# A rebuilt prologue in a fused attention and feed-forward kernel: load order, mask by matmul, a first stage begun operand by operand

## The chip, the cores and the metric

The kernel runs on one core of one Trainium2 chip. The metric is the device time of one execution in microseconds (us); lower is better. The span of a profile is the time from the first to the last instruction of one execution, about 2 us less than the device time. All runs compared below are fast; one run of the kernel before was slow and is left out.

The engines are PE (matmul), PEld (its weight loads), DVE (vector), ACT (scalar), POOL (GpSimd) and SP (which only issues DMA here). "Granted clock" is the share of full speed at which PE was allowed to run. PSUM is the memory in which this kernel keeps the tiles that its matmuls write.

## The reference, cut to what matters

There are 8 batches, 8 heads, 576 positions and a head size of 64. Attention is the sum of two parts: one over positions averaged in fours, and a local one over a band of seven positions. A feed-forward network with a gated activation follows.

```python
q_d = q.reshape(B, H, S // 4, 4, D).mean(axis=3)       # k_d and v_d alike
out_up = np.repeat(softmax(scale * q_d @ k_d.T) @ v_d, 4, axis=2)
mask = np.abs(pos[:, None] - pos[None, :]) < 4
out_local = softmax(np.where(mask, scale * q @ k.T, -1e9)) @ v
x = (out_up + out_local).transpose(0, 2, 1, 3).reshape(4608, 512)
h = x @ w_in                                            # 512 -> 2048
return (h * sigmoid(1.702 * h)) @ w_out                 # 2048 -> 512
```

## The kernel before

The kernel works in nine groups of 512 tokens. Each group runs `mm1` (64 `hps` matmuls with w_in), then `mm2` (64 `ops` matmuls with w_out), and the attention of the next batch is woven into those matmuls. Batch 0 has no group to hide in: its attention is the prologue, and everything up to the first full-speed `hps` matmul is exposed.

v is loaded by the SP queue in ten transfers of 128 KB, each made of rows of 64 floats, which is 256 bytes. q, k and both weights are loaded by the GpSimd queue, with a cast to bf16.

```python
def load_v(b, gate=None):
    t = ldp.tile([128, 5, H, D], FP32, name="vf", tag="vf")
    ...
    for i in range(5):
        for par in range(2):
            nc.sync.dma_start(out=t[64 * par : 64 * par + 64, i],
                in_=bass.AP(tensor=v.tensor, offset=...,
                            ap=[[D, 64], [S * D, H], [1, D]]))
```

v is issued first. GpSimd pools q and k itself and casts half of v, and issues the rest of the weights only behind that.

```python
load_v(0)
load_qk(0, 0)
...
pool_qk(0, 0)                       # GpSimd averages k and q in fours
sp = scores(0, 0)                   # local scores, 80 matmuls
exp_local(0, sp)
...
load_w_in(0, 512)
sd = scores_d(0, 0)                 # pooled scores, 24 matmuls
exp_down(0, sd)
mask_local(0)                       # multiply by the mask on DVE
...
prep_v(0, nc.scalar, ...); prep_v(0, nc.vector, ...); prep_v(0, nc.gpsimd, ...)
load_w_in(512, 512); load_w_in(1024, 1024); ...; load_w_out(0)
...
for hp in range(4):
    x[hp] = transp(y[hp])           # three PSUM buffers in turn
    merge(0, hp, x[hp], copy_od(x[hp]), ...)   # writes xT, the input of mm1
load_v(1, gate=gate)
```

An output tile leaves PSUM through one of three `osb` buffers and is stored by the SP queue, which also loads v.

The softmax here doesn't subtract the row's maximum and nothing guards it: scores larger than these inputs give would overflow.

Of the kernel before, what the change touches and what calls it, by code (L numbers as in the profile page):

```python
# [19 lines left out]
def kernel(  # L20
# [31 lines left out]
    psA = ctx.enter_context(  # L52
        tc.tile_pool(name="psA", bufs=3, space=bass.MemoryType.PSUM)
    )
    psM = ctx.enter_context(
        tc.tile_pool(name="psM", bufs=2, space=bass.MemoryType.PSUM)
# [13 lines left out]

    wz = consts.tile([128, 512], BF16, name="wz")
    psel = consts.tile([128, 7, 64], BF16, name="psel")
# [40 lines left out]
    def make_mask():  # L113
        nc.vector.tensor_tensor(out=dm, in0=dm, in1=dm, op=ALU.mult)
        nc.vector.tensor_single_scalar(out=dm, in_=dm, scalar=9.5, op=ALU.is_lt)
        nc.scalar.copy(
            out=mask.rearrange("p x (i c) -> p (x i) c", c=60),
            in_=dm[:, None, :].to_broadcast([128, 10, 60]),
        )
# [167 lines left out]
    def ps_tile(name):  # L287
        return psA.tile([128, 2, 512], FP32, name=name, tag="psA")

    def scores(b, qd):  # L290
        sp = [ps_tile("sl0"), ps_tile("sl1")]
        for i in range(5):
            for a in range(2):
                for par in range(2):
                    for r in range(4):
# [7 lines left out]
                            start=(a == 0), stop=(a == 1),  # L303
                            tile_position=(32 * r, 64 * par),
                        )
        return sp

    def scores_d(b, qd, sd=None):
        sd = sd or ps_tile("sd")
        for kc in range(3):  # L310
            for a in range(2):
                for r in range(4):
                    rows = slice(32 * r, 32 * r + 32)
                    j = r % 2
                    nc.tensor.matmul(  # L315
                        sd[64 * j : 64 * j + 64, r // 2, SD * kc : SD * kc + SD],
                        lhsT=kdT[qd][rows, 48 * kc : 48 * kc + 64, a],
                        rhs=qdT[b, qd][rows, :, a],
                        start=(a == 0), stop=(a == 1),
                        tile_position=(32 * r, 64 * j),  # L320
                    )
        return sd
# [19 lines left out]
    def av(b, hp):  # L342
        o = ps_tile("av")
# [51 lines left out]
    def transp(y):  # L395
        x = ps_tile("xt")
# [64 lines left out]
    def warm(n):  # L461
        if n:
            t = psM.tile([128, 512], FP32, name="warm", tag="psM")
# [5 lines left out]
    def attention(b):  # L469
# [19 lines left out]
        def avn(*hps):  # L489
            def f():  # L490
                for hp in hps:
                    st["o", hp] = av(b, hp)
# [4 lines left out]
        def tr(*hps):  # L497
            def f():
                for hp in hps:
                    st["x", hp] = transp(st["y", hp])  # L500
# [6 lines left out]


    def mm1(g, steps):
        tok0 = g * TG  # L510
        gT = moe_sb.tile([128, n_ffc, TG], BF16, name="gT", tag="gT")
        for ffc in range(n_ffc):
            for f in steps.get(ffc, ()):
                f()
            hps = psM.tile([128, TG], FP32, name="hps", tag="psM")
            for dmc in range(n_dmc):
                nc.tensor.matmul(  # L517
                    hps,
                    lhsT=w_in_bf[:, dmc, ffc * 128 : (ffc + 1) * 128],
                    rhs=xT[dmc][:, tok0 : tok0 + TG],  # L520
                    start=(dmc == 0), stop=(dmc == n_dmc - 1),
                )
            nc.scalar.activation(  # L523
                out=gT[:, ffc, :], in_=hps, func=AF.Silu, scale=GELU_SCALE
            )
        return gT

    def mm2(g, gT, steps):
# [3 lines left out]
        if g == 0:  # L532
            order = [(t0 + u, c * 4 + f) for t0 in (0, 2) for c in range(4)
# [16 lines left out]
        for t, ffc in order:  # L550
# [5 lines left out]
            if ffc == 0:  # L556
                ops[t] = psM.tile([128, d_model], FP32, name="ops", tag="psM")
# [9 lines left out]
        if g == n_groups - 1:  # L567
            for h in range(2):
                cols = slice(256 * h, 256 * h + 256)
                p = psM.tile([128, d_model], FP32, name="ops", tag="psM")  # L570
# [151 lines left out]
```

## Time and profile before

| | before |
|---|---|
| device time, median of 3 | 336.61 us (334.76 to 338.91) |
| profiled span | 336.2 us |
| PE busy, mean granted clock | 94%, 0.974 |
| first y (a head pair's attention result) | 22.54 us |
| last xT (input of the first stage) complete | 31.47 us |
| first mm2 matmul | 45.96 us |
| group 1's first hps matmul | 74.34 us |
| group 1's first mm2 matmul | 89.58 us |

The first view is the page of the kernel before. Its first line gives busy time, share of the span and number of instructions of each engine. The others cut the span into 40 slices of 8.4 us each; a digit is the busy share, or the granted clock, in tenths.

```profile
PE 315.9 (94%) x5013; PEld 157.4 (47%) x5013; DVE 135.3 (40%) x217; ACT 184.2 (55%) x315; POOL 138.6 (41%) x164
...
PE   6777993999999999999999999999999999999995
...
PEclk9699996799999999999999999999999999999999
DMA  8899992199991897199519951898180010011012
```

PE is full from the eighth slice on. All that a new prologue can win lies in the first eight, where PE is at 0.6 to 0.9 and once at 0.3, and the clock falls twice. The busy time there is not all useful: it includes dummy `warm` matmuls on zeros, whose results nothing reads.

The next view is the table by stretches of the kernel before. Its columns are the stretch in us, its length, busy us and number of instructions of PE, PEld, DVE, ACT and POOL, the granted clock, the DMA share and GB/s.

```profile
10.00:12.50 2.50, 2.14 (x103) 1.59 (x106) 1.26 (x1) 1.23 (x2) 2.10 (x3) 0.78 1.20 220
12.50:15.00 2.50, 2.42 (x98) 1.18 (x88) 2.38 (x3) 1.00 (x2) 2.42 (x3) 0.50 0.84 151
15.00:17.50 2.50, 2.50 (x21) 0.91 (x23) 2.50 (x3) 1.12 (x2) 2.42 (x4) 0.50 0.05 8
20.00:25.00 5.00, 3.53 (x149) 2.28 (x145) 2.67 (x5) 2.08 (x2) 2.62 (x5) 1.00 1.17 189
50.00:55.00 5.00, 0.01 (x1) 0.04 (x1) 0.00 (x0) 0.08 (x1) 1.06 (x1) 0.74 0.49 80
```

DMA is busy until about 14.5 us, nearly idle from 15 to 17.5 us, then busy again. From 50 to 55 us PE does nothing.

The last view is the timeline of the kernel before: start, us from the first start to the last end, engine and line, operation, output and inputs, count, and in brackets the idle time ahead and what ended it.

```profile
0.74 12.28 SPq L174 DMA_DIRECT2D vf<-in_v_dram  x10
...
16.23 0.80 POOL L196 DMA_DIRECT2D w_in_bf<-in_moe_w_in_dram  x1
...
17.04 0.93 PE L315 MATMUL sd<-qdT_281,kdT_98 32*64 32x144 bf16 x24
...
22.54 1.09 DVE L389 TENSOR_TENSOR y<-av,rc 128x896 bf16<-128x896 f32 x1
...
30.51 0.75 DVE L446 TENSOR_TENSOR xT_85<-xt,od 128x570 bf16<-128x570 f32 x1 [0.22 <-ACT od L425]
...
53.94 2.32 POOL L251 CAST vb_87<-vf 128x2560 bf16<-128x2560 f32 x1 [13.12 <-DMA vf<-in_v_dram]
...
56.32 1.71 PE L272 MATMUL vdp<-vb_87,psel 128*64 128x256 bf16 x14 [6.31 <-POOL vb_87 L251]
```

v is issued at 0.74 us and w_in at 16.23 us. The PE stall of 6.31 us waits for v of batch 1, which landed at 53.9 us behind the weights.

### The profile page before, as it was taken

How to read it: one execution, taken by the hardware profiler on the slowest of the kernel's cores; microseconds unless marked ns; L12 is line 12 of the kernel's file. 1: busy time of each engine (PE TensorE's matmuls, PEld its weight loads, DVE VectorE, ACT ScalarE, POOL GpSimd, SP SyncE). 2: the span in 40 equal slices, each digit the busy share in tenths (PEclk: the TensorE clock that was granted, in tenths of full speed). 3: DMA queues.
4: the chain of work that ended last, by engine and by line, in shares of the span. 5: the costliest groups of instructions: out<-in, count | busy, mean ns of one | idle time of the engine just before them, and what ended most of it. 6: DMA issues, size and time to landing. Idle time of an engine off the chain costs nothing.

```text
span 336.2 us, 11213 instructions
## 1 busy us (share of the span) xinstructions
PE 315.9 (94%) x5013; PEld 157.4 (47%) x5013; DVE 135.3 (40%) x217; ACT 184.2 (55%) x315; POOL 138.6 (41%) x164
## 2 busy tenths in 40 slices
PE   6777993999999999999999999999999999999995
PEld 2343442454545455545554545455545554444444
DVE  5766710384067506750675066506750570000000
ACT  2346760546664667466746673668366737424611
POOL 6966802027940892089208920793079000000000
PEclk9699996799999999999999999999999999999999
DMA  8899992199991897199519951898180010011012
GB/s 148 150 159 211 196 200 42 67 181 198 262 190 68 164 204 139 64 181 204 120 67 188 204 114 66 161 208 135 66 163 13 33 67 31 2 63 62 0 55 71
DMA packets 63552, 41.36 MB, mean 123 GB/s; under 512 B 44048, under 2 KB 54416, under 8 KB 63504
## 3 DMA queue, kind: packets, MB, share of 16 engines
q1 hardware_dynamic: 55056, 26.95, 37.5%
q0 software_dynamic: 8304, 13.63, 23.0%
q8 instruction: 39, 0.64, 0.8%
q14 instruction: 9, 0.07, 0.1%
q10 hardware_dynamic: 144, 0.07, 0.1%
HBM read 44.83 MB, written 9.44 MB: 161 GB/s over the span
## 4 chain that ended last, share of the span: by engine, by line
PE 84%; SPq 5%; DMA 4%; POOL 2%; DVE 2%; issue 1%; ACT 1%; POOLq 0%; ACTq 0%
PE ops L558 36%; PE hps L517 33%; SPq L174 5%; DMA qb_128<-in_q_dram 2%; PE sd L315 2%; PE av L354 2%; PE xt L403 2%; PE av L376 2%; DMA vf<-in_v_dram 1%; PE ops L572 1%; PE vdp L272 1%; POOL vb_87 L251 1%; PE warm L465 1%; DVE y L389 1%; PE xt L413 0%
## 5 line engine op out<-in xcount | busy, mean ns | idle before, releaser
L558 PE MATMUL ops<-w_out_bf,gT 128*128 128x512 bf16 x560 | 129.8, 383 | 0.0
L523 ACT ACTIVATE gT<-hps 128x512 bf16<-128x512 f32 x144 | 86.0, 597 | 49.0 <-PE hps L517 49.0
L517 PEld LDWEIGHTS <-w_in_bf 128*128 128x128 bf16 x576 | 55.8, 98 | 68.4 <-issue 2.0
L558 PEld LDWEIGHTS <-gT 128*128 128x128 bf16 x560 | 52.2, 98 | 60.8 <-issue 2.1
L517 PE MATMUL hps<-xT_85,w_in_bf 128*128 128x512 bf16 x144 | 54.6, 379 | 0.8 <-DVE vf L590 0.8
L517 PE MATMUL hps<-xT_82,w_in_bf 128*128 128x512 bf16 x144 | 54.6, 379 | 0.0
L517 PE MATMUL hps<-xT_84,w_in_bf 128*128 128x512 bf16 x144 | 54.6, 379 | 0.0
L517 PE MATMUL hps<-xT_83,w_in_bf 128*128 128x512 bf16 x144 | 54.6, 379 | 0.0
L543 ACT ACTIVATE osb<-ops 128x512 f32<-128x512 f32 (+2 forms) x37 | 22.0, 595 | 40.4 <-PE ops L558 27.2
L340 DVE TENSOR_TENSOR es_90<-es_90,mask 128x600 bf16<-128x600 bf16 x8 | 7.6, 950 | 84.8 <-ACT es_90 L326 84.8
L425 ACT COPY od<-xt 128x384 f32<-128x384 f32 x64 | 21.1, 412 | 36.3 <-PE xt L413 30.8
L389 DVE TENSOR_TENSOR y<-av,rc 128x896 bf16<-128x896 f32 x32 | 34.9, 1092 | 1.1
L545 DVE TENSOR_SCALAR osb<-ops 128x128 f32<-128x128 f32 x1 | 0.3, 291 | 55.3 <-ACT osb L543 55.3
L387 DVE RECIPROCAL rc<-av 128x14 f32<-128x14 f32 x32 | 7.7, 240 | 19.6 <-PE av L376 19.6
L465 PE MATMUL warm<-wz 128*128 128x512 bf16 x41 | 14.1, 476 | 1.2 <-DVE wz L100 1.2
L251 POOL CAST vb_87<-vf 128x2560 bf16<-128x2560 f32 x4 | 9.4, 2344 | 13.1 <-DMA vf<-in_v_dram 13.1
L403 PEld LDWEIGHTS <-y 60*64 60x64 bf16 x640 | 7.4, 107 | 9.2 <-issue 4.3
L403 PE MATMUL xt<-ident,y 60*64 60x57 bf16 (+1 forms) x640 | 9.5, 194 | 1.3 <-issue 0.8
L340 DVE TENSOR_TENSOR es_92<-es_92,mask 128x600 bf16<-128x600 bf16 x8 | 4.2, 529 | 13.8 <-ACT es_92 L326 13.8
L482 ACT ACT_TABLE_LOAD x7 | 9.0, 1283 | 0.1
L478 ACT ACT_TABLE_LOAD x7 | 9.0, 1283 | 0.1
L446 DVE TENSOR_TENSOR xT_84<-xt,od 128x570 bf16<-128x570 f32 x8 | 6.0, 754 | 7.1 <-ACT od L425 7.1
(335 smaller groups left out, 382.5 us busy)
## 6 DMA issues: line engine op xcount, KB each, us to landing
vf<-in_v_dram SPq DMA_DIRECT2D x80, 128.0 KB, 6.6
out_dram<-osb SPq DMA_DIRECT2D x35, 256.0 KB, 2.1
v_96<-in_v_dram SPq DMA_DIRECT2D x36, 192.0 KB, 5.4
w_out_bf<-in_moe_w_out_dram POOLq DMA_DIRECT2D x4, 512.0 KB, 18.0
w_in_bf<-in_moe_w_in_dram POOLq DMA_DIRECT2D x2, 512.0 KB, 6.6
w_in_bf<-in_moe_w_in_dram POOLq DMA_DIRECT2D x1, 1024.0 KB, 11.6
kb_116<-in_k_dram POOLq DMA_DIRECT2D x1, 288.0 KB, 5.3
qb_118<-in_q_dram POOLq DMA_DIRECT2D x1, 288.0 KB, 6.7
```

Source lines behind the costliest of these rows:

```text
L174: nc.sync.dma_start(out=t[64 * par : 64 * par + 64, i], in_=bass.AP(tensor=v.tensor, offset=v[b, 0].offset + (114 * i + KSTART[par]) * D, ...
L251: cp(out=vbs[b % 2][:, i, h, 0:D], in_=vf[b][:, i, h])
L340: nc.vector.tensor_tensor(out=ev, in0=ev, in1=mask, op=ALU.mult)
L389: nc.vector.tensor_tensor(out=y, in0=ov[:, :, :, 0:D], in1=rc.to_broadcast([128, 2, 7, D]), op=ALU.mult,)
L403: nc.tensor.matmul(x[64 * j : 64 * j + 64, par, 57 * i + c0 : 57 * i + c1], lhsT=y[64 * pos : 64 * pos + 60, par, i, :], rhs=ident[64 * po ...
L425: nc.scalar.copy(out=od[:, 4 * t0 : 4 * (t0 + n)].rearrange("p (t f) -> p t f", f=4), in_=x[:, xx, 288 : 288 + n, None].to_broadcast([128, ...
L465: nc.tensor.matmul(t, lhsT=wz[:, 0:128], rhs=wz, start=True, stop=True)
L478: nc.scalar.preload_act_table_set("exp_and_others")
L517: nc.tensor.matmul(hps, lhsT=w_in_bf[:, dmc, ffc * 128 : (ffc + 1) * 128], rhs=xT[dmc][:, tok0 : tok0 + TG], start=(dmc == 0), stop=(dmc = ...
L523: nc.scalar.activation(out=gT[:, ffc, :], in_=hps, func=AF.Silu, scale=GELU_SCALE)
L543: eng.activation(out=osb, in_=ap, func=AF.Copy, scale=1.0 / GELU_SCALE)
L558: nc.tensor.matmul(ops[t], lhsT=gT[:, ffc, t * 128 : (t + 1) * 128], rhs=w_out_bf[:, ffc, :], start=(ffc == 0), stop=(ffc == n_ffc - 1),)
```

## The change

The intent is to make the first stage start earlier and to take out the stall near 50 us. q and k are loaded first, and v waits for the first q tile. For batch 0, the local mask is added to the scores by matmuls instead of multiplied in by DVE, and q is not pooled: the pooled scores come from four accumulating matmuls over its four strided quarters. The weights are issued as soon as GpSimd has averaged the second k tile. v of batch 1 comes before half of w_out. Six `hps` tiles of the first stage begin with the operands that are ready, and the first `mm2` runs over four PSUM accumulators at once. The diff, cut to its core:

```diff
-    load_v(0)
     load_qk(0, 0)
...
     prep_1("q", 0, 0)
-    pool_qk(0, 0)
-    sp = scores(0, 0)
+    load_v(0, gate=after_q)                 # v waits for the first q tile
+    pool_qk(0, 0, "k")
+    sp = scores(0, 0, barred=True)          # mask added by bar_others(), 8 matmuls
     exp_local(0, sp)
     prep_qk(0, 1)
-    pool_qk(0, 1)
+    pool_qk(0, 1, "k")
     load_w_in(0, 512)
...                                          # from below, behind prep_v, to here:
     load_w_in(512, 512)
     load_w_in(1024, 1024)
     for qd in range(NQ):
         load_qk(1, qd)
     load_w_out(0)
+    load_w_out(1)
...
-    sd = scores_d(0, 0)
+    sd = scores_d(0, 0, pooled=False)       # 96 matmuls instead of 24
     exp_down(0, sd)
-    mask_local(0)
...
+    for i in range(5):
+        prep_v(0, nc.vector, i=slice(i, i + 1))
...
+    turned(0)                               # transp + merge, all through PSUM slot 2
+    y[2] = normalise(av(0, 2, 0))
+    part((0, 1), 0)                         # two hps tiles, operand 0
+    turned(1)
+    y[3] = normalise(av(0, 3, 1))
+    part((0, 1), 1)
+    turned(2)
+    part((2, 3), 0, 1)
+    part((0, 1), 2)
+    turned(3)
+    part((4, 5), 0, 1)
+    part((2, 3, 4, 5), 2)
+    part(range(6), 3)
...
-            order = [(t0 + u, c * 4 + f) for t0 in (0, 2) for c in range(4)
+            order = [(t0 + u, 4 * c + f)
+                     for t0, c in ((0, 0), (0, 1), (2, 0), (2, 1),
+                                   (0, 2), (2, 2), (0, 3), (2, 3))
                      for u in range(2) for f in range(4)]
```

The unpooled scores read q like this:

```diff
+        q_of = [qdT[b, qd]] if pooled else [
+            qT[b, qd].rearrange("p (t f) a -> p t f a", f=4)[:, :, f, :]
+            for f in range(4)
+        ]
```

A row of qT holds two bf16 values per position, and a matmul takes one of the two.

More of the change, by code (lines that the diff above doesn't have):

```diff
@@ L51 @@
     moe_sb = ctx.enter_context(tc.tile_pool(name="moe_sb", bufs=1))
-    psA = ctx.enter_context(
-        tc.tile_pool(name="psA", bufs=3, space=bass.MemoryType.PSUM)
-    )
-    psM = ctx.enter_context(
-        tc.tile_pool(name="psM", bufs=2, space=bass.MemoryType.PSUM)
+    psum = ctx.enter_context(
+        tc.tile_pool(name="psum", bufs=1, space=bass.MemoryType.PSUM)
     )
@@ L69, with ps_tile, pm_tile @@
     kdT = [persist.tile([128, 160, 2], BF16, name=f"kdT{i}") for i in range(NQ)]
+    PA = [psum.tile([128, 2, 512], FP32, name=f"pa{i}") for i in range(3)]
+    PM = [psum.tile([128, 512], FP32, name=f"pm{i}") for i in range(2)]
+    turn = {"a": 0, "m": 0}
+    def ps_tile(n=None):
+        if n is None:
+            n = turn["a"] % 3
+            turn["a"] += 1
+        return PA[n]
+    def pm_tile():
+        turn["m"] += 1
+        return PM[turn["m"] % 2]
     wz = consts.tile([128, 512], BF16, name="wz")
+    off = consts.tile([128, 60], BF16, name="off")
     psel = consts.tile([128, 7, 64], BF16, name="psel")
@@ L115, in make_mask @@
         nc.vector.tensor_single_scalar(out=dm, in_=dm, scalar=9.5, op=ALU.is_lt)
+        nc.vector.tensor_scalar(
+            out=off, in0=dm, scalar1=-1.0, scalar2=1e6, op0=ALU.add, op1=ALU.mult
+        )
         nc.scalar.copy(
@@ L284, in prep_vd_pe, with bar_others, scores @@
         )
-    def ps_tile(name):
-        return psA.tile([128, 2, 512], FP32, name=name, tag="psA")
-    def scores(b, qd):
-        sp = [ps_tile("sl0"), ps_tile("sl1")]
+    def bar_others(sp):
+        for par in range(2):
+            rows = slice(64 * par, 64 * par + 64)
+            for r in range(4):
+                nc.tensor.matmul(
+                    sp[r // 2][rows, r % 2, 0:300],
+                    lhsT=ident[rows, :],
+                    rhs=off[rows, None, :].to_broadcast([64, 5, 60]),
+                    start=True, stop=True,
+                    tile_position=(64 * par, 64 * par),
+                    skip_group_check=True,
+                )
+    def scores(b, qd, barred=False):
+        sp = [ps_tile(), ps_tile()]
+        if barred:
+            bar_others(sp)
         for i in range(5):
@@ L302, in scores, with scores_d @@
                             rhs=qT[b, qd][rows, q0 : q0 + 60, a],
-                            start=(a == 0), stop=(a == 1),
+                            start=(a == 0 and not barred),
+                            stop=(a == 1 or barred),
                             tile_position=(32 * r, 64 * par),
+                            skip_group_check=barred,
                         )
         return sp
-    def scores_d(b, qd, sd=None):
-        sd = sd or ps_tile("sd")
-        for kc in range(3):
-            for a in range(2):
-                for r in range(4):
-                    rows = slice(32 * r, 32 * r + 32)
-                    j = r % 2
-                    nc.tensor.matmul(
-                        sd[64 * j : 64 * j + 64, r // 2, SD * kc : SD * kc + SD],
-                        lhsT=kdT[qd][rows, 48 * kc : 48 * kc + 64, a],
-                        rhs=qdT[b, qd][rows, :, a],
-                        start=(a == 0), stop=(a == 1),
-                        tile_position=(32 * r, 64 * j),
-                    )
+    def scores_d(b, qd, pooled=True):
+        sd = ps_tile()
+        q_of = [qdT[b, qd]] if pooled else [
+            qT[b, qd].rearrange("p (t f) a -> p t f a", f=4)[:, :, f, :]
+            for f in range(4)
+        ]
+        last = len(q_of) - 1
+        for kc in range(3):
+            for f, qq in enumerate(q_of):
+                for a in range(2):
+                    for r in range(4):
+                        rows = slice(32 * r, 32 * r + 32)
+                        j = r % 2
+                        nc.tensor.matmul(
+                            sd[64 * j : 64 * j + 64, r // 2, SD * kc : SD * kc + SD],
+                            lhsT=kdT[qd][rows, 48 * kc : 48 * kc + 64, a],
+                            rhs=qq[rows, :, a],
+                            start=(a == 0 and f == 0), stop=(a == 1 and f == last),
+                            tile_position=(32 * r, 64 * j),
+                        )
         return sd
@@ L340, in mask_local, with av @@
             nc.vector.tensor_tensor(out=ev, in0=ev, in1=mask, op=ALU.mult)
-    def av(b, hp):
-        o = ps_tile("av")
+    def av(b, hp, n=None):
+        o = ps_tile(n)
         av_local(b, hp, o)
@@ L393, in normalise, with transp @@
         return y
-    def transp(y):
-        x = ps_tile("xt")
+    def transp(y, n=None):
+        x = ps_tile(n)
         for i in range(5):
@@ L462, in warm @@
         if n:
-            t = psM.tile([128, 512], FP32, name="warm", tag="psM")
+            t = pm_tile()
             for _ in range(n):
@@ L467, in warm, with attention @@
                 )
-    def attention(b):
+    def attention(b, slots=None):
         st = {}
@@ L490, in f @@
             def f():
-                for hp in hps:
-                    st["o", hp] = av(b, hp)
+                for n, hp in enumerate(hps):
+                    st["o", hp] = av(b, hp, slots and slots[n])
                 for hp in hps:
@@ L498, in f @@
             def f():
-                for hp in hps:
-                    st["x", hp] = transp(st["y", hp])
+                for n, hp in enumerate(hps):
+                    st["x", hp] = transp(st["y", hp], slots and slots[n])
                 for hp in hps:
@@ L506, in attention, with hps_mm, new_gT, silu @@
         return [lambda: s_pe(0), lambda: s_act(0), s1, avn(0, 1), avn(2, 3), tr(0, 1), tr(2, 3)]
-    def mm1(g, steps):
-        tok0 = g * TG
-        gT = moe_sb.tile([128, n_ffc, TG], BF16, name="gT", tag="gT")
-        for ffc in range(n_ffc):
+    def hps_mm(g, ffc, dmc, acc):
+        nc.tensor.matmul(
+            acc,
+            lhsT=w_in_bf[:, dmc, ffc * 128 : (ffc + 1) * 128],
+            rhs=xT[dmc][:, g * TG : g * TG + TG],
+            start=(dmc == 0), stop=(dmc == n_dmc - 1),
+        )
+    def new_gT():
+        return moe_sb.tile([128, n_ffc, TG], BF16, name="gT", tag="gT")
+    def silu(gT, ffc, acc):
+        nc.scalar.activation(
+            out=gT[:, ffc, :], in_=acc, func=AF.Silu, scale=GELU_SCALE
+        )
+    def mm1(g, gT, steps, first=0):
+        for ffc in range(first, n_ffc):
             for f in steps.get(ffc, ()):
                 f()
-            hps = psM.tile([128, TG], FP32, name="hps", tag="psM")
+            hps = pm_tile()
             for dmc in range(n_dmc):
-                nc.tensor.matmul(
-                    hps,
-                    lhsT=w_in_bf[:, dmc, ffc * 128 : (ffc + 1) * 128],
-                    rhs=xT[dmc][:, tok0 : tok0 + TG],
-                    start=(dmc == 0), stop=(dmc == n_dmc - 1),
-                )
-            nc.scalar.activation(
-                out=gT[:, ffc, :], in_=hps, func=AF.Silu, scale=GELU_SCALE
-            )
-        return gT
+                hps_mm(g, ffc, dmc, hps)
+            silu(gT, ffc, hps)
     def mm2(g, gT, steps):
@@ L556, in mm2 @@
             if ffc == 0:
-                ops[t] = psM.tile([128, d_model], FP32, name="ops", tag="psM")
+                ops[t] = PA[0][:, t - 2, :] if g == 0 and t > 1 else pm_tile()
             nc.tensor.matmul(
@@ L569, in mm2 @@
                 cols = slice(256 * h, 256 * h + 256)
-                p = psM.tile([128, d_model], FP32, name="ops", tag="psM")
+                p = pm_tile()
                 for ffc in range(n_ffc):
@@ L586, with after_q, after_w_out @@
     POS = [13, 16, 33, 42, 53, 62, 71]
-    POS_0 = [14, 16, 34, 48, 56, 64, 72]
+    POS_0 = [14, 16, 24, 48, 66, 56, 76]
     gate = lambda t: nc.vector.memset(t, 0.0)
     o, y, x = {}, {}, {}
-    load_v(0)
+    def after_q(t):
+        nc.vector.tensor_copy(out=t, in_=qf[0, 0][0:1, 0:1])
+    def after_w_out(t):
+        nc.vector.tensor_copy(out=t, in_=w_out_bf[0:1, 0, 0:1])
+    nc.scalar.preload_act_table_set("exp_and_others")
     load_qk(0, 0)
-    nc.scalar.preload_act_table_set("exp_and_others")
-    iota_psel()
     load_qk(0, 1)
     iota_mask()
+    iota_psel()
     fill()
     warm(17)
-    make_psel(dp, dr)
     make_mask()
+    make_ident(di)
     prep_1("k", 0, 0)
     prep_1("q", 0, 0)
-    pool_qk(0, 0)
-    sp = scores(0, 0)
+    load_v(0, gate=after_q)
+    pool_qk(0, 0, "k")
+    sp = scores(0, 0, barred=True)
     exp_local(0, sp)
     prep_qk(0, 1)
-    pool_qk(0, 1)
+    pool_qk(0, 1, "k")
     load_w_in(0, 512)
-    warm(3)
-    sd = scores_d(0, 0)
-    exp_down(0, sd)
-    mask_local(0)
-    warm(2)
-    sp = scores(0, 1)
-    exp_local(1, sp)
-    mask_local(1)
-    make_ident(di)
-    warm(5)
-    sd = scores_d(0, 1)
-    exp_down(1, sd)
-    prep_v(0, nc.scalar, i=slice(0, 2), h=slice(0, 4))
-    prep_v(0, nc.vector, i=slice(2, 5), h=slice(0, 4))
-    prep_v(0, nc.gpsimd, h=slice(4, 8))
     load_w_in(512, 512)
@@ L630, with part, turned @@
     load_w_out(0)
+    load_w_out(1)
+    make_psel(dp, dr)
+    sd = scores_d(0, 0, pooled=False)
+    exp_down(0, sd)
     warm(2)
+    sp = scores(0, 1, barred=True)
+    exp_local(1, sp)
+    sd = scores_d(0, 1, pooled=False)
+    exp_down(1, sd)
+    nc.scalar.preload_act_table_set("silu_and_others")
+    for i in range(5):
+        prep_v(0, nc.vector, i=slice(i, i + 1))
+    warm(4)
+    prep_vd_pe(0, PA[2])
     for hp in range(2):
-        o[hp] = ps_tile("av")
+        o[hp] = PA[hp]
         av_local(0, hp, o[hp])
-    prep_vd_pe(0, ps_tile("vdp"))
-    nc.scalar.preload_act_table_set("silu_and_others")
-    warm(2)
-    for hp in range(4):
-        if hp < 2:
-            av_down(0, hp, o[hp])
-        else:
-            o[hp] = av(0, hp)
-        y[hp] = normalise(o[hp])
-    warm(2)
-    for hp in range(4):
-        x[hp] = transp(y[hp])
-        merge(0, hp, x[hp], copy_od(x[hp]), eng=nc.gpsimd if hp < 2 else None)
-        warm(2)
-    load_v(1, gate=gate)
-    for c in range(1, 4):
-        load_w_out(c)
+    for hp in range(2):
+        av_down(0, hp, o[hp])
+        y[hp] = normalise(o[hp])
+    warm(4)
+    gT0 = new_gT()
+    turn["m"] = 0
+    acc = PM + [PA[n][:, u, :] for n in range(2) for u in range(2)]
+    def part(ffcs, *dmcs):
+        for dmc in dmcs:
+            for ffc in ffcs:
+                hps_mm(0, ffc, dmc, acc[ffc])
+    def turned(hp):
+        x[hp] = transp(y[hp], 2)
+        merge(0, hp, x[hp], copy_od(x[hp]))
+    turned(0)
[11 more added lines that the diff above has]
+    part(range(6), 3)
+    for ffc in range(6):
+        silu(gT0, ffc, acc[ffc])
     def loads_2():
-        load_qk(2, 0, gate=gate)
-        load_qk(2, 1)
-        load_v(2)
+        load_v(2, gate=gate)
         load_v4(2)
@@ L661 @@
         if g == 0:
-            prep_1("k", 1, 0)
-            prep_1("q", 1, 0)
+            prep_qk(1, 0)
             pool_qk(1, 0)
@@ L666 @@
             pool_qk(1, 1)
+            load_v(1, gate=after_w_out)
             nc.vector.memset(v4[32:64], 0.0)
-            prep_v(1, nc.gpsimd)
+            prep_v(1, nc.gpsimd, i=slice(0, 4))
+            load_w_out(2)
+            load_w_out(3)
+            prep_v(1, nc.gpsimd, i=slice(4, 5))
+            for qd in range(NQ):
+                load_qk(2, qd)
         elif b < B:
@@ L684 @@
         if b < B:
-            for n, f in zip(POS if g else POS_0, attention(b)):
+            for n, f in zip(POS if g else POS_0, attention(b, None if g else (1, 2))):
                 steps.setdefault(n, []).append(f)
             if g == 0:
-                steps[POS_0[2]].insert(0, lambda: prep_vd_pe(1, ps_tile("vdp")))
-                steps[POS_0[3]].append(loads_2)
-        gT = mm1(g, steps)
+                steps.setdefault(45, []).append(lambda: prep_vd_pe(1, PA[2]))
+                steps[POS_0[5]].append(loads_2)
+        gT = new_gT() if g else gT0
+        mm1(g, gT, steps, 0 if g else 6)
         mm2(g, gT, {n - 16: f for n, f in steps.items() if n >= 16})
```

## The prediction

> **What bounds the kernel now.** The span is 336.2 us, PE busy 94%. From 74.4 us on, the chain of waits is almost only PE: six groups of about 33.8 us, then 58.8 us. The change leaves them alone. All there is to win lies before 74.4 us, where group 1's matmuls start.
>
> The timeline and the table by stretches show four costs there. (1) The last xT comes at 31.5 us; only 3 of group 0's 128 matmuls ran before it. (2) DMA limits what is below: its share is about 1.1 from 2.5 to 14.5 us (q, k, v of batch 0), near 0 to 17.5 because GpSimd issues w_in only at 16.2, then 1.0 to 1.25 until v of batch 1 lands at 53.7. (3) PE idles 50.0 to 56.3 us for the cast vb_87 of that v. (4) The granted clock is then 0.50 to about 62 us: fourteen ops matmuls take 4.5 us, not 3.0. (3) and (4) cost about 9 us. [...]
>
> **What the change does.** It loads q/k first, v behind them; the mask goes into PSUM by 16 matmuls, so four multiplications (5.2 us of VectorE) go; q is not pooled for batch 0 (144 more sd matmuls, 23 to 39 ns each, in PE slack). The w_in issue moves from 16.2 to about 11.5 us. v of batch 1 comes before half of w_out, so it should land near 45 us: (3) and (4) should vanish. Over six hps tiles, 18 matmuls run before the last xT: 15 x 0.216 = 3.2 us won.
>
> VectorE still makes y and xT of four head pairs in series (4 x 1.35 + 4 x 1.0 us), through one PSUM slot, and v lands at 17 to 18 us, so the last xT comes at 30 to 32 us, as before. Six SiLUs in a row (0.6 us each) then hold PE about 1.5 us. The second score step, moved to 8 matmuls into mm2, waits for table load and exponentials: 1.8 us.
>
> **The new wait.** Group 0 now finishes all four output tiles within its last 13 matmuls. From n=40 the SP queue first issues v and v4 of batch 2: 16 issues of at least 0.5 to 0.6 us, 10 to 14 us in all. The first store stands behind them; the fourth osb reuses its buffer (there are three) and stands ahead of all SiLUs of group 1. From that gate to the end of mm2 are about 4.6 us; PE can do two more hps tiles (1.7 us), then waits until the store has landed (2.1 us). I estimate 6.5 to 10 us of PE idle, then about 3 us of slow clock.
>
> **Sum.** Last xT 30.5 + 110 x 0.216 + attention 6.2 + small waits 4 + new wait 8 + clock 3 = 75.5 us, against 74.4. The stall is moved, not removed. My new wait may be too large, so I shade it down.
>
> Predicted: 335.0 us, range 328.0 to 340.0; faster by over 2%: 0.22, within 2%: 0.73, slower by over 2%: 0.05.
>
> **What would show it.** Right: no PE idle for vb near 50 us; first mm2 matmul at 41 to 45 us (46.0 before); ACT's fourth osb waits for the out DMA; PE idles over 5 us after group 1's second hps tile; clock near 0.5 after it; later groups 33.5 us each. Wrong: group 1 flows without that gap (325 to 329 us), or vdp or w_out still stalls mm2.
>
> **What would make it wrong.** v issues faster than 0.5 us each; v of batch 0 landing at 14 us, everything 3 us earlier; the clock low during the split hps matmuls (slower).

The sum comes to 75.5 us: 30.5 + 23.8 + 6.2 + 4 + 8 + 3. The last term, 3 us of slow clock, is an estimate that fits the trace before: after its stall PE ran at a clock of 0.50 for about 6 us (56.3 to 62.5 us), and half of that is lost.

## The result, and the profile after

The changed kernel took 368.15 us (367.23 to 368.45, four runs), the kernel before 337.53 us in the same rounds. The ratio is 1.091, with a 95% interval of 1.086 to 1.097: 9% slower. A ratio here and below is the record's, from the fast runs of the same rounds, so it is not quite the ratio of the medians quoted. The record has no mark of correctness for this run; e1 to e3, which leave its arithmetic as it is, are marked correct. The range of the prediction, 328 to 340 us, missed it by 28 us.

The page after, in slices of 9.1 us:

```profile
PE 329.8 (90%) x5159; PEld 164.4 (45%) x5159; DVE 133.0 (36%) x222; ACT 181.7 (50%) x312; POOL 130.2 (36%) x156
...
PE   8990579899259999999999999999999999999996
...
PEclk9665568999859999999999999999999999999999
DMA  7899400597999017941992497179418011002002
```

There are two holes in PE: slices 4 to 5 (0 and 5), and slices 11 to 12 (2 and 5). DMA is full in the first hole and idle right after it.

The table by stretches after, with the same columns:

```profile
15.00:20.00 5.00, 5.00 (x127) 2.71 (x123) 0.43 (x1) 2.12 (x3) 2.88 (x5) 0.58 1.23 204
...
30.00:35.00 5.00, 0.00 (x0) 0.00 (x0) 0.00 (x0) 0.00 (x0) 0.00 (x0) 0.50 1.16 200
...
40.00:45.00 5.00, 3.31 (x86) 1.97 (x85) 1.92 (x4) 0.80 (x1) 0.00 (x0) 0.50 0.03 6
95.00:105.00 10.00, 0.00 (x0) 0.00 (x0) 2.56 (x3) 1.13 (x3) 9.76 (x12) 0.64 1.10 227
```

From 30 to 35 us no engine works while DMA moves 200 GB/s. From 95 to 105 us PE does nothing. The clock is at 0.50 in and after the first hole and at 0.64 in the second.

The timeline after:

```profile
9.12 6.33 PE L350 MATMUL pa<-qT,kdT 32*64 32x144 bf16 x96
...
11.70 2.36 POOL L211 DMA_DIRECT2D w_in_bf<-in_moe_w_in_dram  x3
...
15.30 0.43 DVE L266 CAST vb<-vf 128x512 bf16<-128x512 f32 x1 [1.53 <-DMA vf<-in_v_dram]
...
26.40 0.43 DVE L266 CAST vb<-vf 128x512 bf16<-128x512 f32 x1 [10.67 <-DMA vf<-in_v_dram]
...
36.25 0.43 DVE L266 CAST vb<-vf 128x512 bf16<-128x512 f32 x1 [9.42 <-DMA vf<-in_v_dram]
...
41.02 0.43 DVE L266 CAST vb<-vf 128x512 bf16<-128x512 f32 x1 [4.33 <-DMA vf<-in_v_dram]
...
43.74 1.09 DVE L424 TENSOR_TENSOR y<-pa,rc 128x896 bf16<-128x896 f32 x1
...
56.18 0.75 DVE L481 TENSOR_TENSOR xT<-pa,od 128x570 bf16<-128x570 f32 x1 [2.38 <-ACT od L460]
...
103.87 0.60 ACT L585 ACTIVATE osb<-pa 128x512 f32<-128x512 f32 x1 [11.96 <-DMA out_dram<-osb]
105.00 1.44 PE L544 MATMUL pm<-xT,w_in_bf 128*128 128x512 bf16 x3 [10.55 <-ACT gT L555]
```

The five casts of v's slices tell the story of the first hole. The second was done at 15.7 us; the third, fourth and fifth waited for their data until 26.4, 36.3 and 41.0 us. w_in had been issued at 11.70 us, between the first request for v and its landing. In the second hole the fourth output tile waits for a buffer whose store has not landed (11.96 us), and PE waits for ACT behind it (10.55 us).

The time from one milestone to the next shows where the 29 us came from:

| stage | before, us | after, us | difference |
|---|---|---|---|
| start to first y | 22.54 | 43.74 | +21.2 |
| first y to last xT complete | 8.93 | 13.40 | +4.5 |
| last xT to first mm2 matmul | 14.49 | 12.78 | -1.7 |
| first mm2 matmul to group 1's first hps | 28.38 | 21.70 | -6.7 |
| group 1's first hps to its first mm2 | 15.24 | 28.19 | +12.9 |
| sum | 89.58 | 119.81 | +30.2 |

The spans differ by 29.2 us; the later groups take 33.4 to 34.4 us each in both kernels. So the intended gains are there (the rows with -1.7 and -6.7), and they are outweighed by three losses.

### The profile page after: what moved, and what is told of

The parts are those of the page before. It is cut to its first block, busy times and chain, and to the rows that moved or that the text cites. A ratio compares the mean times of both kernels' runs of the same rounds, so it can differ in the third digit from the quotient of the medians.

```text
span 365.4 us, 11482 instructions
## 1 busy us (share of the span) xinstructions
PE 329.8 (90%) x5159; PEld 164.4 (45%) x5159; DVE 133.0 (36%) x222; ACT 181.7 (50%) x312; POOL 130.2 (36%) x156
## 4 chain that ended last, share of the span: by engine, by line
PE 77%; DMA 10%; SPq 5%; ACT 3%; DVE 2%; issue 1%; POOL 0%; DVEq 0%; ACTq 0%; POOLq 0%
PE pm L544 33%; PE pm L600 30%; DMA vf<-in_v_dram 6%; SPq L189 4%; PE pa L326 3%; PE pa L438 2%; DMA out_dram<-osb 2%; PE pa L350 2%; PE pa L389 2%; PE pa L411 2%; DMA qb<-in_q_dram 1%; ACT gT L555 1%; DVE xT L481 1%; PE pa L544 1%; PE pa L600 1%
## 5 line engine op out<-in xcount | busy, mean ns | idle before, releaser
L544 PE MATMUL pm<-xT,w_in_bf 128*128 128x512 bf16 x560 | 127.3, 384 | 14.5 <-ACT gT L555 11.1
L600 PE MATMUL pm<-w_out_bf,gT 128*128 128x512 bf16 x528 | 121.3, 380 | 0.0
L555 ACT ACTIVATE gT<-pm 128x512 bf16<-128x512 f32 x140 | 83.3, 598 | 48.9 <-PE pm L544 48.9
L544 PEld LDWEIGHTS <-w_in_bf 128*128 128x128 bf16 x576 | 56.3, 99 | 84.3 <-issue 20.6
L460 ACT COPY od<-pa 128x384 f32<-128x384 f32 x64 | 21.1, 411 | 40.8 <-DVE y L424 22.2
L585 ACT ACTIVATE osb<-pm 128x512 f32<-128x512 f32 (+2 forms) x35 | 20.7, 593 | 40.2 <-PE pm L600 28.3
L424 DVE TENSOR_TENSOR y<-pa,rc 128x896 bf16<-128x896 f32 x32 | 34.9, 1091 | 1.1
L481 DVE TENSOR_TENSOR xT<-pa,od 128x570 bf16<-128x570 f32 x32 | 24.1, 753 | 16.3 <-ACT od L460 16.3
L361 ACT ACTIVATE es<-pa 128x600 bf16<-128x600 f32 x32 | 19.7, 668 | 6.8 <-PE pa L326 6.3
L272 POOL TENSOR_TENSOR v<-v 112x512 f32<-112x512 f32 x18 | 22.8, 1267 | 0.0
L235 DVE STREAM_TRANSPOSE kT<-kb 128x576 f32<-128x576 f32 x16 | 19.9, 1246 | 0.9 <-DMA kb<-in_k_dram 0.9
L235 DVE STREAM_TRANSPOSE qT<-qb 128x576 f32<-128x576 f32 x16 | 19.8, 1238 | 0.2
L367 ACT ACTIVATE ed<-pa 128x864 bf16<-128x864 f32 x16 | 14.3, 896 | 9.9 <-PE pa L350 9.9
L251 POOL TENSOR_TENSOR pq<-qT 128x576 f32<-128x576 bf16 x14 | 16.1, 1147 | 0.0
L350 PEld LDWEIGHTS <-kdT 32*64 32x64 bf16 x528 | 13.6, 114 | 4.2
## 6 DMA issues: line engine op xcount, KB each, us to landing
w_in_bf<-in_moe_w_in_dram POOLq DMA_DIRECT2D x1, 1024.0 KB, 14.5
```

The costliest lines, as they stand in the source:

```text
L235: nc.vector.transpose(out=t32.rearrange("p (i c) -> p c i", c=18), in_=store[b, qd].bitcast(FP32).rearrange("p (c d) -> p c d", c=18),)
L251: nc.gpsimd.tensor_tensor(out=t1, in0=sv[:, :, 0:2, :], in1=sv[:, :, 2:4, :], op=ALU.add)
L272: eng.tensor_tensor(out=t1[0:112], in0=x[:, :, 0:2, :], in1=x[:, :, 2:4, :], op=ALU.add)
L350: nc.tensor.matmul(sd[64 * j : 64 * j + 64, r // 2, SD * kc : SD * kc + SD], lhsT=kdT[qd][rows, 48 * kc : 48 * kc + 64, a], rhs=qq[rows, : ...
L424: nc.vector.tensor_tensor(out=y, in0=ov[:, :, :, 0:D], in1=rc.to_broadcast([128, 2, 7, D]), op=ALU.mult,)
L460: nc.scalar.copy(out=od[:, 4 * t0 : 4 * (t0 + n)].rearrange("p (t f) -> p t f", f=4), in_=x[:, xx, 288 : 288 + n, None].to_broadcast([128, ...
```

## The experiments

The theories, for each hole.

First hole. Theory S: v is starved. Its small rows on the SP queue share the DMA engines with 4.5 MB of bulk on the GpSimd queue, and get a small part. The rivals: v is late of itself, because it is requested behind q and k, in small packets, by ten issues on SP (T); or PE is late because of its 192 pooled-score matmuls, which take 66 ns each where 23 to 39 ns were predicted.

Second hole. Theory W: the first store stands in the SP queue behind sixteen issues for batch 2, and a fourth osb buffer would cure it. The rival: SP and DMA are simply too late there, so that another wait takes its place.

The twelve runs came in three sets, each with its own seven runs of the kernel before: e1 to e4, e5 to e8 and e9 to e12. The first set ran on another chip than the other two, so results of different sets are compared by their ratios. Diffs are against the changed kernel unless the text says otherwise.

### e1_gate: the weights wait for v

```diff
     pool_qk(0, 1, "k")
+    vgate = consts.tile([128, 5], FP32, name="vgate")
+    nc.gpsimd.tensor_copy(out=vgate, in_=vf[0][:, :, 0, 0])
     load_w_in(0, 512)
```

GpSimd copies one value of each slice of v, so its weight loads are issued only when v has landed (from 20.25 us in this run, after the last wait for v at 19.74 us). Everything else stays.

> The changed kernel, with one tiny GpSimd copy that reads the first column of all five slices of v of batch 0, put ahead of the first w_in issue: the bulk loads start only when v has landed. Theory S (v, issued second on another queue, is starved of DMA by the 4.5 MB of w_in, q/k of batch 1 and w_out queued behind it): v lands by 18 us instead of 41, the first y starts near 27 us instead of 43.5 (the unpooled sd matmuls then end last, near 24.6 us), and the time falls by about 16 us, to 349 to 356. Rival T (v is slow of itself: late gate, small packets, ten issues on SP): v still lands after 30 us and the time stays within 1% of 368.

Measured: 354.55 us, ratio 1.051 (1.045 to 1.056), span 352.7 us. The timeline of this run shows v in by 19.7 us, and y 14.3 us earlier than in the changed kernel:

```profile
17.47 0.43 DVE L266 CAST vb<-vf 128x512 bf16<-128x512 f32 x1 [1.11 <-DMA vf<-in_v_dram]
19.74 0.43 DVE L266 CAST vb<-vf 128x512 bf16<-128x512 f32 x1 [1.84 <-DMA vf<-in_v_dram]
...
29.44 1.09 DVE L424 TENSOR_TENSOR y<-pa,rc 128x896 bf16<-128x896 f32 x1
```

v was still requested behind q and k, so the order of the requests is not what cost 21 us. Holding back the bulk alone brought v in 21 us earlier and shortened the span by 12.7 us. v and y both came about 2 us later than expected. And y came 9.7 us after v, not 2.7 us as before the gate. The pooled-score matmuls, which had been hidden, are now in the way; e4 tests that.

### e2_osb4: a fourth output buffer

```diff
-            osb = moe_sb.tile([128, n], FP32, name="osb", tag=f"osb{n}", bufs=3)
+            osb = moe_sb.tile([128, n], FP32, name="osb", tag=f"osb{n}", bufs=4)
```

> The changed kernel with four output buffers in place of three, so that the fourth output copy of group 0 need not wait for the first store, which stands behind 16 loads on the SP queue. Theory W (that buffer is what holds PE from 94.5 to 105 us): the gap of 10.6 us and about 1.5 to 3 us of half clock behind it go, time 354 to 358. Rival: PE is then held by something else at the same place (v of batch 2 late, stores piling up at the next group), and the time falls by less than 5 us.

Measured: 357.64 us (354.71 to 358.11), ratio 1.058 (1.052 to 1.064), span 352.9 us. The same stretches of this run, first the timeline, then the table:

```profile
92.03 10.74 PE L544 MATMUL pm<-xT,w_in_bf 128*128 128x512 bf16 x48 [0.49 <-DVE xT L487]
```

```profile
95.00:105.00 10.00, 9.89 (x145) 4.91 (x145) 1.38 (x2) 6.04 (x11) 9.76 (x12) 1.00 1.07 220
```

The second hole is gone, and with it 12.5 us of the profiled span: 10.55 us of idle and about 2 us of slow clock (0.70 from 105 to 110 us in the changed kernel; 1.00 in the table above). DMA carries the same load there, so it was the buffer and not the DMA rate. The profiled run was the fastest of the four; by medians the gain is 10.5 us.

### e3_gate_osb4: both

The two edits above together.

> Both edits. If the two costs are independent, their savings add: 368 - 16 - 12 = 340, range 335 to 345. If the second gap only reappears elsewhere once the first part is faster, 348 or more.

Measured: 340.68 us, ratio 1.011 (1.005 to 1.017), span 338.7 us. The spans add up within 1.5 us: 365.4 less 12.7 less 12.5 is 340.2. By medians the two gains of 13.6 and 10.5 us give 24.1 us, and both together gave 27.5 us. The two holes are separate, and they are nearly all of the loss. What is left is 1% over the kernel before.

### e4_gate_osb4_pooled: q pooled again

On top of e3:

```diff
-    pool_qk(0, 0, "k")
+    pool_qk(0, 0)
...
-    sd = scores_d(0, 0, pooled=False)
+    sd = scores_d(0, 0)
...                                          # and the same for (0, 1)
```

> Both edits, and q of batch 0 is pooled on GpSimd again, 24 sd matmuls in place of 96 per head group. The 96 took 5.1 to 6.4 us each time in the changed kernel's trace, about 64 ns a matmul. Theory P (once v is in time, they are what the first y waits for): sd is over by 17 us, the first y starts near 21 us instead of 27, time 5 to 7 us below the run with both edits, 332 to 335. Rival (they lie in PE slack, as I predicted): within 2 us of that run.

Where this says 5.1 to 6.4 us, the trace of the changed kernel has 6.33 and 6.38 us for its two 96s, 66 ns a matmul.

Measured: 334.97 us, ratio 0.992 (0.988 to 0.997), span 333.6 us. The timeline of e3, then that of e4:

```profile
9.01 6.33 PE L350 MATMUL pa<-qT,kdT 32*64 32x144 bf16 x96
...
18.08 6.38 PE L350 MATMUL pa<-qT,kdT 32*64 32x144 bf16 x96
```

```profile
10.85 0.58 PE L350 MATMUL pa<-qdT,kdT 32*64 32x144 bf16 x24 [1.70 <-POOL qdT L260]
...
14.88 0.58 PE L350 MATMUL pa<-qdT,kdT 32*64 32x144 bf16 x24 [1.51 <-POOL qdT L260]
...
22.97 1.09 DVE L424 TENSOR_TENSOR y<-pa,rc 128x896 bf16<-128x896 f32 x1
```

Four times the matmuls took eleven times the time. Pooled, PE waits 3.2 us for GpSimd and still finishes 9 us sooner; the first y comes at 22.97 us instead of 29.64 us. This is worth 5.7 us by medians, but only once v is in time: in the changed kernel v came last anyway.

### e5_vfirst: v first, bulk not held back

The fourth buffer, and v requested ahead of q and k as before:

```diff
+    load_v(0)
     load_qk(0, 0)
...
-    load_v(0, gate=after_q)
```

> The changed kernel with four output buffers, and v of batch 0 issued first, ungated, as in the kernel before; w_in is not held back. Theory S (v loses to the bulk loads only because it is still in flight when they start at 12.5 us): v lands by 16 us, time near that of the run with gate and four buffers (340.7), 337 to 345. If the early w_in still starves v's tail, v lands at 20 to 30 us and the time lies between 345 and 357.

Measured: 340.78 us, ratio 1.008 (1.004 to 1.013), span 340.0 us, as fast as e3. Four slices of v were cast by 16.1 us; the fifth, still on its way when the bulk was issued (from 12.84 us), came at 20.65 us, as late as the second theory of the expectation had it, but the time is that of the first. Either remedy serves: bulk behind v by a gate, or v far enough ahead.

### e6_samequeue: v on the queue of the bulk (inconclusive)

The fourth buffer, and v issued by GpSimd between q/k and the weights:

```diff
-                nc.sync.dma_start(
+                (q or nc.sync).dma_start(
...
     iota_mask()
+    load_v(0, q=nc.gpsimd)
```

> The changed kernel with four output buffers, and v of batch 0 issued by GpSimd on the queue that also carries q/k and, behind it, w_in. Nothing is gated. If the loss lies in the sharing between two queues, order within one queue cures it: v lands by 20 us although w_in is queued right behind it, time 340 to 350 (GpSimd pools q/k some 5 us later, which costs). If it lies in v's small packets as such, v lands after 30 us and the time is 355 or more.

Measured: 348.34 us, ratio 1.031 (1.025 to 1.037). This run decides nothing about the queue. GpSimd's ten issues of v (4.4 to 13.1 us) put off its own pooling of k; the pooled scores ran only at 17.1 and 26.2 us, the first y came at 37.5 us. w_in was issued only at 19.07 us, when v was nearly in. So the bulk never met v.

### e7_bulk_over_v: the load order alone, in the kernel before

This is the kernel before, with nothing of the change but the order of the first loads: v behind the first q tile, and the weights right after.

```diff
-    load_v(0)
     load_qk(0, 0)
...
     prep_1("q", 0, 0)
+    load_v(0, gate=lambda t: nc.vector.tensor_copy(out=t, in_=qf[0, 0][0:1, 0:1]))
+    load_w_in(0, 512)                       # these lines come from below
+    load_w_in(512, 512)
+    load_w_in(1024, 1024)
+    for qd in range(NQ):
+        load_qk(1, qd)
+    load_w_out(0)
     pool_qk(0, 0)
```

> The kernel before, with only the order of its first loads changed: q/k first, v of batch 0 on SP gated behind q, and w_in, q/k of batch 1 and the first quarter of w_out issued by GpSimd right behind q/k, ahead of its pooling. Nothing else of the change. Theory S: this alone costs most of the loss: v lands after 35 us, the first y near 40 us instead of 22.5, time 350 to 360. If v lands before 25 us and the time stays below 343, the order of loads is not enough to explain the loss.

Measured: 351.28 us, ratio 1.040 (1.033 to 1.046). v was in at about 36.6 us, the first y came at 41.70 us against 22.54 us. The line of y in its timeline:

```profile
41.70 1.09 DVE L389 TENSOR_TENSOR y<-av,rc 128x896 bf16<-128x896 f32 x1
```

So the load order makes the first hole without the rest of the change. The loss in time, 13.3 us by medians (351.28 less 337.96), is less than the 19 us at the first y; this kernel took 8.9 us from first y to last xT, as the kernel before did, and part of the rest comes back at the stall near 50 us: PE waits 1.6 us there instead of 6.3 us, and from the first mm2 matmul to group 1 it takes 22.8 us instead of 28.4 us.

### e9_same_queue: the same, with v on the queue of the bulk

Against e7, one edit: the ten transfers of v are issued by GpSimd, ahead of the bulk. It moves two more things with it: v is first requested at 5.92 us instead of 8.48 us, and the bulk, which waits for GpSimd to issue v, at 13.23 us instead of 5.92 us.

```diff
-    load_v(0, gate=lambda t: nc.vector.tensor_copy(out=t, in_=qf[0, 0][0:1, 0:1]))
+    load_v(0, q=nc.gpsimd)
```

> The kernel before with the same bulk loads pulled ahead as in the run that lost 13 us (351.3, v landed at about 36), but v of batch 0 goes through GpSimd's own queue, ahead of them, in place of the SP queue. Theory Q (the loss lies in two queues sharing the DMA engines, and order within one queue cures it): v lands by 20 us though 4.5 MB are queued right behind it; GpSimd issues for longer and pools q/k later, so the first y comes near 28 us instead of 41, time 337 to 343. Rival (256-byte rows make v slow whatever the queue): v lands after 28 us, 347 or more.

Measured: 341.76 us, ratio 1.015 (1.011 to 1.019). This time the bulk followed right behind v. The DMA view of the stretch from 5 to 40 us, first of e7, then of e9. A queue's line gives packets, MB and share of the 16 engines' time; an issue's line gives the count, the size of one and the median time from issue to landing.

```profile
DMA packets 8371, 5.95 MB, mean 170 GB/s; under 512 B 5459, under 2 KB 6995, under 8 KB 8369
...
q0 software_dynamic: 3089, 4.61, 73.9%
q1 hardware_dynamic: 5280, 1.31, 23.8%
...
vf<-in_v_dram SPq DMA_DIRECT2D x10, 128.0 KB, 9.9
```

```profile
DMA packets 3576, 5.99 MB, mean 171 GB/s; under 512 B 339, under 2 KB 1875, under 8 KB 3572
...
q0 software_dynamic: 3572, 5.93, 94.9%
...
vf<-in_v_dram POOLq DMA_DIRECT2D x10, 128.0 KB, 6.3
```

The bytes and the rate are the same. But in e7 a transfer of v took 9.9 us from issue to landing by the median and in e9 6.3 us; v was in at about 19 us instead of 36.6 us. In e7 the SP queue also got its ten requests out only by 33.5 us, in 25.0 us; in e9 they were out by 13.2 us, in 7.3 us. The number of packets fell by 4,795 because v's 5,280 packets of about 248 bytes became about 490 packets of about 2.7 KB, ten rows each. That fits Q and speaks against the rival of the expectation, that rows of 256 bytes are slow on any queue. It does not separate three readings: within a queue v stands ahead of the bulk; its packets are larger; and most of v was under way before the bulk was requested at all, as in e5, where v on the SP queue was in at 20.65 us. So it is not shown that the queue is the cure. Here too the first y was late (33.98 us), because GpSimd's issues put off its pooling; this is no version to keep.

### e10_contiguous_q: the stride of q (wrong result)

On top of e3, the four quarters of q are read contiguously. The scores are then wrong, and numbers and shapes of matmuls are unchanged. (The record marks the run as correct all the same, so its check did not see this error in batch 0.)

```diff
-            qT[b, qd].rearrange("p (t f) a -> p t f a", f=4)[:, :, f, :]
+            qT[b, qd].rearrange("p (f t) a -> p t f a", f=4)[:, :, f, :]
```

> Wrong result on purpose. The changed kernel with gate and four output buffers (340.7); the 96 sd matmuls per head group read q in four contiguous quarters in place of every fourth column. In all runs so far the 96 took 6.33 to 6.38 us, whatever the clock, 66 ns a matmul, against 24 to 39 ns of the pooled ones. Theory (the stride of the moving operand costs): they now take 2.3 to 3.8 us, and the time falls by 3 to 6 us, to 335 to 338. Rival (the number and the clock alone): still over 5 us, time within 2 us of 340.7.

Measured: 334.82 us, ratio 0.995 (0.988 to 1.003), against 1.011 for e3. The timeline, to be held against the first line of e3 above:

```profile
8.76 1.73 PE L350 MATMUL pa<-qT,kdT 32*64 32x144 bf16 x96
```

96 matmuls take 1.73 us instead of 6.33 us, 18 ns each instead of 66 ns. So it is the stride of the moving operand that costs, not the number of matmuls. The strided time was 6.33 to 6.38 us in the changed kernel, in e3 and in e6, and hardly followed the granted clock: the trace of the changed kernel has 20 to 24 of these matmuls in each us at a clock of 1.00 (9.2 to 12.2 and 19.3 to 22.3 us), and 20 to 24 at 0.50 (12.6 to 14.6 and 23.3 to 24.3 us). The time of the pooled, closely read ones did: 24 took 0.93 us at 0.50 (17.04 us in the kernel before) and 0.59 us at 1.00 (67.66 us in the changed kernel). e10's second 96 came in two stretches, 60 in 1.17 us and 36 in 1.29 us, 20 and 36 ns each.

### e8_all: v first, bulk held back, fourth buffer, q pooled

The edits of e4 and of e5 together.

> The changed kernel with v first, w_in held until v has landed, four output buffers and pooled q: what is left of the change is the mask in PSUM, the split first matmuls, the order of v before w_out and the four accumulators. v lands by 15 us, the first y at 20 to 21 us (22.7 with v behind q), time 331 to 333, against 335.0 with v behind q. If the time is within 1 us of 335, something other than v sets the first y by then.

Measured: 332.76 us, ratio 0.984 (0.978 to 0.989), span of the kept profile 329.8 us. v was in at 16.35 us, the first y came at 19.87 us and the last xT was complete at 32.57 us. That is 12.7 us after the first y, where the kernel before needs 8.9 us. The transposes of four head pairs go through one PSUM slot, and PE works on parts of the first stage between them.

### e11_reordered and e12_two_slots: the chain from y to xT

e11 is e8 with each transpose ahead of the partial matmuls that stood before it, and one step of the next attention moved back by four `mm2` matmuls. e12 also gives the last transpose a slot of its own, with the accumulators of the first stage moved to slots 1 and 2:

```diff
     turned(0)
     y[2] = normalise(av(0, 2, 0))
-    part((0, 1), 0)
     turned(1)
+    part((0, 1), 0)
     y[3] = normalise(av(0, 3, 1))
-    part((0, 1), 1)
     turned(2)
+    turned(3, 0)                            # PSUM slot 0; e11 keeps slot 2
+    part((0, 1), 1)
     part((2, 3), 0, 1)
     part((0, 1), 2)
-    turned(3)
     part((4, 5), 0, 1)
```

> The run with v first, gate, four buffers and pooled q (332.8), with PE's transposes of one head pair put ahead of the split hps matmuls that wait for the same xT, and the second score step at 12 in place of 8 matmuls into mm2. There the last xT came at 32.4 us, 12.8 us after the first y, with 0.5, 1.1 and 2.4 us of VectorE idle ahead of the last three merges. Expected: 1.5 to 2.5 us of that idle go, and 0.9 us at the scores; time 329 to 331. If the clock stays low there, 332.

> As the reordered run, but the fourth transpose goes to a PSUM slot of its own, so it need not wait for the third merge. Expected: last xT at 29 to 30 us, 1 to 2 us below the reordered run, time 327.5 to 330. If PE and not VectorE sets that chain by then, no change against the reordered run.

Measured: e11 331.68 us, ratio 0.984 (0.981 to 0.988); e12 330.68 us (329.45 to 331.34), ratio 0.981 (0.977 to 0.985). Both are slightly above what was expected. The chain from first y to last xT took 11.7 us in e11. In e12 it is 9.0 us again, and xT is complete at 29.02 us, 3.6 us before e8. By medians only about 2 us of it reached the end, and even that is not clear of noise: e8 ran in another set, and the intervals of the two ratios overlap. Fewer partial matmuls are done ahead of it, the clock is at 0.80 to 0.86 from 25 to 35 us, and the third quarter of w_out is now late by 0.84 us (1.86 us in e11). The two lines from the timeline of e12:

```profile
28.07 0.75 DVE L481 TENSOR_TENSOR xT<-pa,od 128x570 bf16<-128x570 f32 x1
...
56.45 1.89 PE L600 MATMUL pm<-w_out_bf,gT 128*128 128x512 bf16 x8 [0.84 <-DMA w_out_bf<-in_moe_w_out_dram]
```

e12 is the fastest version that was found: 1.9% under the kernel before, and marked correct.

## Why the prediction was wrong

**The step that failed** is, in the words of the prediction, "v lands at 17 to 18 us, so the last xT comes at 30 to 32 us, as before". v landed at 41.0 us and the last xT was complete at 57.1 us. The term "last xT 30.5" of the sum was too small by about 27 us. An earlier sentence, "The w_in issue moves from 16.2 to about 11.5 us", was right to 0.2 us (11.70 us) and was counted as a gain. It was what starved v: SP had begun all ten issues of v by 17.5 us, but the tenth issue itself took 11.6 us, and between 15 and 36 us one slice of 262 KB took 10 to 11 us, which is about 25 GB/s of the 203 GB/s that DMA moved. e1 shows it by holding back the bulk (v in at 19.7 us) and e7 by making the same hole in the kernel before; e9 agrees, but changes more than the queue. Whether SP's long issues are a cause of the starving or an effect of it is not shown; in the kernel before, where only q and k were in flight beside v, the ten took 12.3 us.

What could have been read beforehand: the prediction notes that DMA is "near 0 to 17.5 because GpSimd issues w_in only at 16.2", and takes the pause for waste. v was in when that pause began; until then the late w_in had left DMA to q, k and v. Up to 14.5 us DMA moved 1.24 MB of v and 1.18 MB of q and k. In the changed kernel v met the bulk: from 8 to 45 us the GpSimd queue took 68.6% of the time of the 16 DMA engines and the SP queue 21.6%, and v slowed down while the total stayed near 200 GB/s (203 from 15 to 36 us). v's 1.31 MB went in 5,280 packets (248 bytes each) and the GpSimd queue's 4.53 MB in 3,323 packets (1,363 bytes each); while v was starved it got about 12% of the bandwidth. Small packets beside larger ones do not account for that alone: in the kernel before, v got roughly half of the bandwidth beside q and k until 14.5 us, in 4,990 packets of about 248 bytes beside 576 of about 2,048 bytes. What sets the shares is not shown, and why the load is not starved there stays open.

**"144 more sd matmuls, 23 to 39 ns each, in PE slack" was wrong too.** They took 66 ns each, 6.3 us per 96, and e10 shows that the stride is the cause: 66 ns where a matmul on quarter f reads 2 bytes in every 16, 18 ns where it reads 2 in every 4, with number and shapes unchanged. By what mechanism the stride costs is not shown. In the changed kernel the wait for v hid this; once v was in time it cost 5.7 us (e3 to e4). So the step would have failed with v in time too: in e3, with v in at 20.2 us, the last xT was complete at 41.8 us.

**The chain from y to xT was mis-sized.** The prediction put four head pairs at about 9.4 us (4 x 1.35 + 4 x 1.0 us). It took 13.4 us, and still 12.7 us in e8 with v in time. With the transposes moved and a second slot (e12) it took 9.0 us. So even with v in at 16.35 us and q pooled (e8), the last xT came at 32.57 us and not at 30.5 us.

**The new wait was right in its path and nearly in its size.** The prediction gave 6.5 to 10 us of PE idle after group 1's second hps tile, then about 3 us of slow clock. Measured were 10.55 us of idle after exactly eight matmuls, two tiles (three at 91.6 us and five at 93.2 us), and a span 12.5 us shorter without it (e2). The chain of waits after names sixteen SP issues (ten of v at L189, six of v4 at L201), 10.2 us in all, and then the store, as predicted. Only the store took longer, 6.3 us where 2.1 us had been put down. From that view (start, us, what), the first issue of each kind and the store:

```profile
87.10 0.59 SPq L189
...
94.27 0.62 SPq L201
...
97.43 6.33 DMA out_dram<-osb
```

The intuition that this wait "may be too large" and the shading down were wrong.

**The gains were right.** The stall of 6.3 us for vb_87 is gone, and with it the slow clock that followed (0.50 from 55 to 60 us before; 1.00 from 70 to 95 us after): the stretch from the first mm2 matmul to group 1 is 6.7 us shorter. The split first stage gave 1.7 us from last xT to the first mm2 matmul; 3.2 us less about 1.5 us for the SiLUs had been predicted. The second score step waits 1.3 us in all, where 1.8 us were predicted. Only the moment was wrong: the first mm2 matmul was to come at 41 to 45 us and came at 69.9 us; in e8, with v in time and q pooled, it came at 44.8 us. What lowers the clock is not shown. In the trace after it was 0.50 from 30 to 40 us, where PE worked for 0.64 of 10 us, and 0.64 from 95 to 105 us, where PE did nothing. But it was also 0.58 from 15 to 20 us, with PE counted as fully busy, in part by the slow strided matmuls; this was not looked into.

Put together, 29 us of loss in the span are 21.2 up to the first y, 4.5 for the chain and 12.9 in group 1, less 1.7 and 6.7 gained, and about 1 us given back later. Of the 21.2 us the gate gave back 14.3 us (e1), and pooled q most of the rest once v was in time (e4: first y at 22.97 us). The prediction had the last loss and the gains, and lacked the first two.

## What to carry to other kernels

A transfer that is requested first need not land first: here v, requested from 8.43 us, was in only at 41.0 us, while the three loads of w_in, issued from 11.70 us, took at most 14.5 us each to land. So when bulk is to be moved forward, ask which critical load is still in flight, and hold the bulk back until that load has landed (v in at 19.7 us, e1). Here it was a load of small rows on another queue; which of the two properties mattered was not separated. A late issue that leaves DMA idle can be what lets a critical load through, as the w_in issue at 16.23 us did here, so before moving it forward, find out what lands ahead of it (e7: v in at 36.6 us once it was moved). More matmuls on a strided operand are not priced by their count: 96 took 6.33 us strided and 1.73 us contiguous (e10). Take the duration from a matmul with the same stride, or measure one.
